# Strassen's seven block products for the second MLP product, with two attention banks and an ELU on pairs of tiles

## The chip, the cores and the metric

The kernel runs on one core of one Trainium2 chip. The metric is the device time of one execution in microseconds (us), smaller is better. The kernel before takes 628.42 us, the median of three runs (627.26 to 628.8). PE is the TensorE matmul engine, PEld its weight loads, DVE the VectorE, ACT the ScalarE, POOL the GpSimd engine.

## The reference

A gated linear attention (batch 4, 8 heads, 768 tokens, head size 48) feeds a two-layer MLP with an ELU between.

```python
f = 1.0 / (1.0 + np.exp(-f_logit))
for t in range(S):
    state = f[:, :, t, :, None] * state + np.einsum('bhd,bhe->bhde', k[:, :, t], v[:, :, t])
    y[:, :, t] = np.einsum('bhd,bhde->bhe', q[:, :, t], state)
x = y.transpose(0, 2, 1, 3).reshape(B * S, H * D)           # 3072 x 384
h = x @ w_in                                                # 384 x 2048
g = np.where(h > 0.0, h, np.exp(np.minimum(h, 0.0)) - 1.0)
out = g @ w_out                                             # 2048 x 384
```

The weights reach the core as float64 values. The kernel converts them to float32 in unit 0, with one step on ACT and three on DVE.

## The kernel before

The 3072 tokens are cut into 12 units of 256. While the MLP of unit m runs, the gates and the attention of unit m+1 are made beside it. The 2048 hidden columns are 16 tiles of 128. Unit 0 is ordered by hand. From unit 1 on a scheduler, which works with modelled durations, decides in which order the instructions stand in each engine's queue; each engine then takes its queue in order. The parts that the change and the argument touch (cuts marked):

```python
def check(n):            # 16 of them: are all weights of this piece in range?
    raw = sb.tile([128, 2 * DM], w_in.dtype, tag="raw", bufs=AHEAD, ...)      # AHEAD = 7
    nc.sync.dma_start(out=raw[:], in_=flat[n // 2])
    for i, op in enumerate((ALU.min, ALU.max)):
        nc.vector.tensor_reduce(out=spans[:, i, n : n + 1], in_=..., op=op, ...)

def decays(u, pairs, cols):                       # gates of unit u: scan, reciprocal, products
    for p in range(pairs.start, pairs.stop):
        nc.vector.tensor_tensor_scan(out=g[:, p, cols], data0=a, data1=restart[...], ...)
    nc.vector.reciprocal(p_[:, pairs, cols], g[:, pairs, cols])
    for e, x, y in ((nc.vector, t["q"], p_), (nc.gpsimd, t["k"], g)):
        e.tensor_tensor(out=x[:, pairs, cols], in0=x[:, pairs, cols], in1=y[:, pairs, cols], op=ALU.mult)

# attention in four PSUM banks: transposes and states in "t", "y"; scores and outputs in "s0", "s1"

def up(T):                                        # first product and ELU of one tile
    ph = ps.tile([128, U], FP32, tag="h", bufs=2)
    for kt in range(NKT):
        nc.tensor.matmul(ph[:], lhsT=wi[:, kt, s * 128 : (s + 1) * 128], rhs=xts[m][:, kt, :], ...)
    nc.scalar.activation(e[:], ph[:], AF.Relu, scale=-1.0)
    nc.scalar.activation(e[:], e[:], AF.Exp, scale=-1.0)
    nc.vector.scalar_tensor_tensor(out=gs[T][:], in0=e[:], scalar=-1.0, in1=ph[:], op0=ALU.add, op1=ALU.max)

def down(T):                                      # second product, in two PSUM banks
    for i in range(NW):
        nc.tensor.matmul(pms[m][i][:], lhsT=g[:, i * 128 : (i + 1) * 128], rhs=wo[:, s, :], ...)

# in the loop over the tiles s of unit m:
            up(T)
            if T >= HLAG:                         # HLAG = 2
                down(T - HLAG)
            next(steps, None)                     # one step of the gates of unit m+1
            if 4 <= m < 8 and s >= NFT - 4:
                check(4 * (m - 4) + s - NFT + 4)
```

The checks guard the conversion: if a weight is out of range, a slow general path follows. The source places them in units 4 to 7, and the scheduler pulls them forward.

## Time and profile before

| | before |
|---|---|
| median of three runs | 628.42 us |
| span of the profiled run | 626.8 us |
| PE busy | 93% of the span |
| DVE busy | 51%, but nearly full until 190 us |
| first ELU of units 0, 1, 2, 3 | 37.9, 102.5, 153.3, 201.6 us |
| steady unit | 47.0 us |

The measure is the length of a unit: the time from the first ELU of one unit to the first ELU of the next, read in DVE's timeline.

PE waits here, but only in short pieces. These are all of PE's waits between 102 and 202 us (start, length, engine, line, group, count, and in brackets the idle time before it and what ended it):

```profile
134.08 1.56 PE L749 MATMUL psH<-xt,wi 128*128 128x256 f32 x6 [1.05 <-DVE gg L757]
144.48 1.56 PE L749 MATMUL psH<-xt,wi 128*128 128x256 f32 x6 [1.15 <-DVE gg L757]
148.00 1.56 PE L749 MATMUL psH<-xt,wi 128*128 128x256 f32 x6 [0.67 <-DVE gg L757]
193.64 1.56 PE L749 MATMUL psH<-xt,wi 128*128 128x256 f32 x6 [1.00 <-DVE gg L757]
```

### The profile page before, as it was taken

The numbers are of one execution on the slowest core, as the hardware profiler recorded it, in microseconds if no ns is written. First come the engines' busy times: TensorE is split into PE (matmuls) and PEld (weight loads), VectorE is DVE, ScalarE is ACT, GpSimd is POOL, SyncE is SP. The second block draws the span as 40 slices with busy tenths as digits, with TensorE's granted clock in tenths as the row PEclk, the third lists the DMA queues.
The fourth block names the chain that finished last, engine by engine and source line by source line (L and its number), as shares of the span: only waits on it lengthen the run. The fifth ranks groups of instructions, "written<-read, shape, count | busy, mean of one in ns | idle before, by whom it ended". The sixth has DMA issues, their size and how long they took to land.

```text
span 626.8 us, 12052 instructions
## 1 busy us (share of the span) xinstructions
PE 584.9 (93%) x4922; PEld 428.7 (68%) x4922; DVE 316.6 (51%) x549; ACT 235.7 (38%) x532; POOL 55.3 (9%) x115
## 2 busy tenths in 40 slices
PE   2774989998999999999999999999999999999995
PEld 1453767766776777777777777777777777777773
DVE  6879899997796192191191192181181131131110
ACT  2252454544444424423423423423423423423332
POOL 7011012320020020020020010010000000000000
PEclk9886899999999999999999999999999999999998
DMA  8999806776772012011011011021000000000000
GB/s 185 225 258 239 203 17 144 153 250 233 268 263 57 25 53 58 26 52 33 25 52 33 25 52 32 27 52 31 27 2 7 25 2 8 27 1 8 27 0 30
DMA packets 31936, 50.71 MB, mean 81 GB/s; under 512 B 3680, under 2 KB 24704, under 8 KB 31872
## 3 DMA queue, kind: packets, MB, share of 16 engines
q1 hardware_dynamic: 31248, 49.26, 29.5%
q8 instruction: 40, 0.66, 0.5%
q10 hardware_dynamic: 624, 0.59, 0.4%
q14 instruction: 24, 0.20, 0.1%
HBM read 44.04 MB, written 4.72 MB: 78 GB/s over the span
## 4 chain that ended last, share of the span: by engine, by line
PE 77%; DVE 10%; DMA 8%; issue 2%; ACT 1%; POOL 1%; DVEq 0%; SPq 0%; POOLq 0%; ACTq 0%
PE psH L749 35%; PE psM L767 34%; DMA raw<-in_moe_w_in_dram 4%; DVE p L555 3%; DMA q<-in_q_dram 2%; DVE g L551 2%; DVE spans L524 2%; PE psS L602 2%; PE psY L639 2%; PE psT L577 2%; DMA f<-in_f_logit_dram 1%; PE psY L656 1%; DVE gg L757 1%; PE psU_t L621 1%; DVE bits L500 1%
## 5 line engine op out<-in xcount | busy, mean ns | idle before, releaser
L749 PE MATMUL psH<-xt,wi 128*128 128x256 f32 x1152 | 287.4, 386 | 11.3 <-DVE gg L757 11.2
L767 PE MATMUL psM<-wo,gg 128*128 128x384 f32 x768 | 281.7, 490 | 0.0
L749 PEld LDWEIGHTS psH<-xt,wi 128*128 128x128 f32 x1152 | 215.3, 191 | 76.7 <-DVE gg L757 19.9
L757 DVE SCALAR_TENSOR_TENSOR gg<-e,psH 128x256 f32<-128x256 f32 x192 | 79.0, 412 | 273.7 <-ACT e L755 273.6
L767 PEld LDWEIGHTS psM<-wo,gg 128*128 128x128 f32 x768 | 147.6, 192 | 62.6 <-issue 1.8
L754 ACT ACTIVATE e<-psH 128x256 f32<-128x256 f32 x192 | 73.6, 383 | 303.5 <-PE psH L749 289.7
L555 DVE RECIPROCAL p<-g 128x256 f32<-128x256 f32 x48 | 82.4, 1734 | 0.5
L755 ACT ACTIVATE e<-e 128x256 f32<-128x256 f32 x192 | 79.9, 416 | 5.9
L557 POOL TENSOR_TENSOR k<-k,g 128x256 f32<-128x256 f32 x48 | 36.3, 778 | 257.3 <-DMA k<-in_k_dram 210.7
L577 PE MATMUL psT<-ident,k 128*128 128x128 f32 x96 | 14.8, 295 | 19.6 <-POOL k L557 19.6
L551 DVE TENSOR_TENSOR_SCAN g<-f,restart 128x256 f32<-128x256 f32 x44 | 29.4, 711 | 2.7 <-POOL f L544 2.7
L524 DVE TENSOR_REDUCE spans<-again 128x1 f32<-128x768 f32 x32 | 28.8, 942 | 0.6 <-DMA again<-in_moe_w_in_dram 0.6
L577 PEld LDWEIGHTS psT<-ident,k 128*128 128x128 f32 x96 | 12.1, 152 | 24.7 <-POOL k L557 20.5
L579 ACT COPY kn<-psT 128x512 f32<-128x512 f32 x24 | 13.1, 588 | 23.0 <-PE psT L577 23.0
L557 DVE TENSOR_TENSOR q<-q,p 128x256 f32<-128x256 f32 x48 | 19.8, 432 | 0.4
L607 DVE TENSOR_TENSOR at<-psS,twice 128x512 f32<-128x512 f32 x22 | 14.1, 685 | 10.0 <-PE psS L602 10.0
L479 ACT ACTIVATE raw<-raw 128x768 int32<-128x768 uint32 x16 | 14.3, 911 | 7.7 <-DMA raw<-in_moe_w_out_dram 6.1
L540 ACT ACTIVATE f<-f 128x512 f32<-128x512 f32 x24 | 14.2, 621 | 6.3 <-DMA f<-in_f_logit_dram 5.7
L500 DVE CUSTOM_DVE_ANT_0 bits<-raw,bits 128x1536 uint16<-128x1536 uint16 x16 | 15.3, 959 | 2.4 <-ACT raw L479 1.6
L543 POOL COPY restart<-f 128x8 f32<-128x8 f32 x22 | 7.3, 332 | 101.2 <-ACT f L541 69.8
L639 PEld LDWEIGHTS psY<-at,v 64*64 64x64 f32 x704 | 11.3, 135 | 6.0 <-issue 2.7
L602 PEld LDWEIGHTS psS<-q,k 48*64 48x64 f32 x704 | 11.3, 134 | 6.0 <-issue 6.0
(65 smaller groups left out, 244.9 us busy)
## 6 DMA issues: line engine op xcount, KB each, us to landing
raw<-in_moe_w_out_dram SPq DMA_DIRECT2D x8, 768.0 KB, 11.6
again<-in_moe_w_in_dram SPq DMA_DIRECT2D x8, 768.0 KB, 6.3
again<-in_moe_w_out_dram SPq DMA_DIRECT2D x8, 768.0 KB, 7.7
v<-in_v_dram SPq DMA_DIRECT2D x12, 384.0 KB, 4.8
raw<-in_moe_w_in_dram SPq DMA_DIRECT2D x16, 288.0 KB, 9.3
out_dram<-o SPq DMA_DIRECT2D x24, 192.0 KB, 1.9
f<-in_f_logit_dram SPq DMA_DIRECT2D x23, 192.0 KB, 4.2
k<-in_k_dram SPq DMA_DIRECT2D x23, 192.0 KB, 4.3
```

What stands on the lines that cost most here:

```text
L524: nc.vector.tensor_reduce(out=spans[:, i, n : n + 1], in_=raw[:].bitcast(FP32)[:, 1::2], axis=mybir.AxisListType.X, op=op, apply_absolute_ ...
L551: nc.vector.tensor_tensor_scan(out=g[:, p, cols], data0=a, data1=restart[:, p, cols] if u else a, initial=1.0, op0=ALU.mult, op1=ALU.max,)
L555: nc.vector.reciprocal(p_[:, pairs, cols], g[:, pairs, cols])
L557: e.tensor_tensor(out=x[:, pairs, cols], in0=x[:, pairs, cols], in1=y[:, pairs, cols], op=ALU.mult)
L577: nc.tensor.transpose(pt[:, p, :], in_=qkf[u % NB]["k"][:, p, w * W : (w + 1) * W], identity=ident[:])
L602: nc.tensor.matmul(pc[r][FULL[b], w, p], lhsT=t["k"][HALF[r], p, cols], rhs=t["q"][HALF[r], p, cols], start=True, stop=True,)
L639: nc.tensor.matmul(pys[u][b][FULL[r ^ b], w, p], lhsT=vs[u % NB][FULL[b], w, h * D : h * D + 64], rhs=at[FULL[b], r, w, p], start=(w == 0 ...
L749: nc.tensor.matmul(ph[:], lhsT=wi[:, kt, s * 128 : (s + 1) * 128], rhs=xts[m][:, kt, :], start=(kt == 0), stop=(kt == NKT - 1),)
L754: nc.scalar.activation(e[:], ph[:], AF.Relu, scale=-1.0)
L755: nc.scalar.activation(e[:], e[:], AF.Exp, scale=-1.0)
L757: nc.vector.scalar_tensor_tensor(out=gs[T][:], in0=e[:], scalar=-1.0, in1=ph[:], op0=ALU.add, op1=ALU.max)
L767: nc.tensor.matmul(pms[m][i][:], lhsT=g[:, i * 128 : (i + 1) * 128], rhs=wo[:, s, :], start=(s == 0), stop=(s == NFT - 1),)
```

## The change

The second product becomes one of blocks: two tiles of the hidden layer times two halves of the 256 tokens, times two halves of the 384 output columns. Strassen's method needs seven block products instead of eight. They are summed over the whole unit in four PSUM banks, and five additions at the end of the unit assemble the output. The seven products need four sums of the activations for each pair of tiles (on DVE) and four combinations of the weights (made once, on DVE; they stand after unit 0 in the source). Units 0 and 1 keep the direct product, because the weights are still arriving. To have four banks, the attention gets two instead of four. To save DVE instructions, the ELU runs on two tiles at once. To save memory, the scan of the gates writes in place over `f`, and the range checks share three buffers of a fixed area. Two more edits come with these: all scans of a unit now stand ahead of its reciprocals, and the five attention groups stand at other tiles than the four before. The diff, cut to its core:

```diff
-    pc = [ps.tile([128, NW, HP, C], FP32, tag=f"s{r}", ...) for r in range(2)]        # scores
+    pc = [ps.tile([128, NW, HP, C], FP32, tag=f"a{r}", ...) for r in range(2)]
-    pu = [ps.tile([128, NW, HP, D], FP32, tag=n, ...) for n in ("t", "y")]            # states
+    pu = [ps.tile([128, NW, HP, D], FP32, tag=n, ...) for n in ("a0", "a1")]
...
-        raw = sb.tile([128, 2 * DM], w_in.dtype, tag="raw", bufs=AHEAD)               # a range check
+        raw = area[:, 4 + n % (AHEAD - 4)]
...
             nc.vector.tensor_tensor_scan(
-                out=g[:, p, cols], data0=a, ...
+                out=a, data0=a, ...
...
-            0: [lambda: transposed(u, 0, "t"), lambda: transposed(u, 1, "y")],
-            2: [lambda: scores(u), lambda: advance(u)],
-            4: [lambda: outputs(u)],
-            7: [lambda: carried(u)],
+            3: [lambda: transposed(u, 0, "a0"), lambda: transposed(u, 1, "a1")],
+            6: [lambda: advance(u)],
+            8: [lambda: scores(u)],
+            10: [lambda: outputs(u)],
+            12: [lambda: carried(u)],
...
+    def up(P):                                    # a pair of tiles
+        ph = ps.tile([128, 2, U], FP32, tag="h", bufs=2)
...
+        if m >= DIRECT:                           # DIRECT = 2
+            a = [[g[:, i, t * 128 : (t + 1) * 128] for i in range(2)] for t in range(2)]
+            for i, x, y, op in (
+                (0, a[1][0], a[1][1], ALU.add), (2, a[0][0], a[1][0], ALU.subtract),
+                (1, s[:, 0], a[0][0], ALU.subtract), (3, a[0][1], s[:, 1], ALU.subtract),
+            ):
+                nc.vector.tensor_tensor(out=s[:, i], in0=x, in1=y, op=op)
...
+        for bank, half, x, y in (
+            (0, 0, a[0][0], b[0][0]), (3, 0, a[0][1], b[1][0]), (2, 1, a[1][1], c[3]),
+            (1, 0, s[:, 0], c[0]), (1, 1, s[:, 2], c[2]), (0, 1, s[:, 1], c[1]), (2, 0, s[:, 3], b[1][1]),
+        ):
+            nc.tensor.matmul(pm[bank][:, half * DH : (half + 1) * DH], lhsT=x, rhs=y, ...)
...
+            add(flat[:, 0:DH], p[3][0], u2[:])    # the assembly, once a unit, five such additions
...
+            if s % 2 == 0:
+                up(P)
+            elif P:
+                down(P - 1)
...
         if m == 0:
             start.close()
+            combine()                             # the four combinations of the weights
```

## The prediction

> **What bounds the kernel now.** I read the page first: busy shares, the 40 slices, the costliest groups.
>
> ```profile
> span 626.8 us, 12052 instructions
> PE 584.9 (93%) x4922; PEld 428.7 (68%) x4922; DVE 316.6 (51%) x549; ACT 235.7 (38%) x532; POOL 55.3 (9%) x115
> ...
> PE   2774989998999999999999999999999999999995
> ...
> DVE  6879899997796192191191192181181131131110
> ```
>
> PE is full from about the fourth slice on, and DVE is full too in the first 10 to 12 slices (to some 190 us), then half idle. So there are two regimes: a start (to about 200 us) in which PE and DVE compete for the bound, and a steady stretch that is PE alone. The groups say what PE does:
>
> ```profile
> L749 PE MATMUL psH<-xt,wi 128*128 128x256 f32 x1152 | 287.4, 386 | 11.3 <-DVE gg L757 11.2
> L767 PE MATMUL psM<-wo,gg 128*128 128x384 f32 x768 | 281.7, 490 | 0.0
> ...
> L757 DVE SCALAR_TENSOR_TENSOR gg<-e,psH 128x256 f32<-128x256 f32 x192 | 79.0, 412 | 273.7 <-ACT e L755 273.6
> ...
> L555 DVE RECIPROCAL p<-g 128x256 f32<-128x256 f32 x48 | 82.4, 1734 | 0.5
> ```
>
> Each product in the program is two records (576 first-layer products, 1152 records). The mean of 490 ns is a latency; the rate is read from the timeline of PE in a steady unit:
>
> ```profile
> 382.54 1.46 PE L749 MATMUL psH<-xt,wi 128*128 128x256 f32 x6
> 383.83 1.45 PE L767 MATMUL psM<-wo,gg 128*128 128x384 f32 x4
> 385.12 1.46 PE L749 MATMUL psH<-xt,wi 128*128 128x256 f32 x6
> ```
>
> Six records start 1.29 us apart from the next group, so 215 ns for 256 columns; four take 1.29 us, so 323 ns for 384 columns. That is 0.84 ns a column plus 1 to 3 ns. A unit (256 tokens, 16 tiles of the hidden layer) is 16 x 2 x 1.294 = 41.4 us and its attention the rest of the 46.98 us period (psH at 502.84 and 549.81 in the chain of waits), so 5.6 us. No wait breaks it. The table by stage shows where that is not so:
>
> ```profile
> 140.00:190.00 50.00, 48.19 (x412) 35.16 (x411) 41.83 (x67) 23.12 (x53) 4.63 (x12) 1.00 0.71 241
> ...
> 340.00:390.00 50.00, 50.00 (x437) 37.05 (x436) 22.24 (x43) 17.68 (x43) 2.89 (x4) 1.00 0.12 35
> ```
>
> (Columns: stretch, length, PE, PEld, DVE, ACT, POOL, clock, DMA share, GB/s.) At 140 to 190 us DVE is busy 41.8 of 50 and PE already loses 2 us. The DVE timeline puts the first ELU of units 0, 1, 2 and 3 at 37.9, 102.5, 153.3 and 201.6 us: 64.6, 50.8 and 48.3 us for the first three units, against 47 us of PE work.
>
> **What the Trainium skill says.** "TensorE: Matmul & The Clock Gate", LDWEIGHTS: loading weights takes about columns/1.2 ns, 107 ns for 128 columns, and Part 2 says that the queue pulls the next load ahead of running matmuls. The trace agrees: eight 128-column transposes, each with weights of its own, take 1.04 us at 112.97, with the next group 0.87 us after their start, so 109 ns each with the load hidden. "VectorE: DVE Perf Modes", the errata section: an fp32 tensor_tensor takes (N+151)/0.96 ns. The trace: 358 ns at N=192 (formula 357), 432 at 256 (424); so I use it for sizes that are not here. "ScalarE: Activation LUTs", What ACT_TABLE_LOAD costs: with immediates, 186 + 0.833 N ns. The trace: 383 and 416 ns at 256 (399), 621 at 512 (613).
>
> **The change part by part.**
> *PE, second product.* A pair of tiles was 4 products of 384 columns, 8 records x 323 = 2.59 us. It becomes 7 products of 192 columns, 14 records of about 160 + 2.7 = 163 ns, 2.28 us. Every product now has its own weights, but a load of 107 ns fits under 163. Saved 0.31 us a pair, 2.5 us a unit, 25 us over the ten units from unit 2 on. Attention has the same products, in five groups instead of four; each switch of tile shape costs about 0.1 us. Steady unit: 16 x 1.294 + 8 x 2.28 + 5.7 = 44.6 us against 46.98; the last unit, without attention, 38.9 against 41.4.
>
> *DVE, steady.* ELU on pairs: 8 of (512+140)/0.96 = 0.68 us for 16 of 0.41, 1.2 us less. Added: 32 sums of 128 columns, 0.29 us each by the formula, 0.25 started back to back (successive DVE rows overlap by 0.07 to 0.09 us in the trace), 8.0 us; the assembly of a unit, five additions, 2.2 us. So a unit goes from about 22 to 31 us of DVE, out of 44.6. I laid the order of instructions of one steady unit against these durations: with reciprocals (1.65 us each) between, the sums of pair 3 are ready at about the time PE wants them and those of pair 4 up to 0.4 us late in some units. The assembly frees the four banks 3.2 us after the last product, and PE wants the first again after a first-layer pair and the transposes, 3.5 us. Tight, but beside PE. ACT: 16 of 0.6 us instead of 32 of 0.4, and small copies: hidden.
>
> *The first units.* Here DVE counts, so I summed DVE by unit, from the first ELU of one to the first ELU of the next, in the order that the scheduler gave, with start-to-start times of the trace (one weight conversion of three steps 2.46, scan 0.60, reciprocal 1.65, q product 0.33, state step 0.39, mask 0.6, range check 0.87, ELU 0.33, on pairs 0.60):
> - Unit 0 before: 12 conversions 29.5, 16 ELU 5.3, 8 scans 4.8, 8 reciprocals 13.2, 8 q 2.6, states and masks 4.3 = 59.7 of 64.6 us. After: two reciprocals and three q later (4.3 less), ELU 0.5 less, and 16 operations that make the four weight combinations, (384+151)/0.96 = 0.56, back to back 0.48 each = 7.6 us: 62.5. The wait of PE for the k product and the transposes (52 to 60.5 us in the trace), behind which ACT stood, goes, because both scans now come first; but DVE was busy there nearly throughout, so it gives back only a part of the 4.9 us of DVE idle. I take 65.5 us: the first ELU of unit 1, now of two tiles, at 103.5.
> - Unit 1 (still direct, PE 47): before 42.5 of DVE in 50.8. After: 10 reciprocals 16.5, 16 scans 9.6, 8 checks 7.0, 8 ELU 4.8, 11 q 3.6, rest 4.1 = 45.6. Both near PE's 47: about 51.5, so 155.
> - Unit 2 (first with seven products, PE 44.5): before 39.8 in 48.3. After: 22 checks 19.1, sums 8.0, 8 scans 4.8, ELU 4.8, reciprocals 6.6, rest 5.4 = 48.7. DVE bounds this unit: the checks of the weights' range, which filled DVE's idle time, now stand beside the sums. They also have three buffers instead of seven (landing 6 to 8 us), which can add a wait or two. About 51, so 206.
> *The end.* From there unit 3 45, 7 x 44.6, 38.9 = 396.1, so 602. The tail: the last pair cannot hide its ELU, the assembly is five dependent steps (about 2.8 us) for one copy of 0.48, and one output of 384 KB instead of two of 192 (1.9 us each); by the times of the tail before, 8.2 us after where the next ELU would be: 610.3. The runs' median is 1.6 us above the span: **612 us**. So about 9 of the 25 us saved are lost: DVE in units 1 and 2, the combinations, and the tail.
>
> **The rivals.**
> *Weights bound the seven products.* Weight loads rise from 8 to 14 a pair, and the mean LDWEIGHTS record is 192 ns, longer than 163. If that were occupancy, 14 x 192 = 2.69 us, more than before, and the kernel would end near 640. Against: the transposes' 109 ns each. Unlikely.
> *DVE stays out of the way.* Were units 1 and 2 as long as PE's work plus the earlier losses (50 and 46), the end comes near 604 to 606. For it: DVE needs no more than PE's time in unit 1. Against: unit 2's sum of 48.7 against 44.5.
> *DVE and banks stall the steady stretch.* If every unit waits 0.5 to 1 us for late sums or for the assembly's banks, 4 to 9 us: 616 to 621. For it: the slack of 0.3 us on the banks and the bunched reciprocals. Against: five of the seven products need no late sum, and the order puts the direct ones first.
> *The transfers.* The loads and the range checks moved to three buffers stand in one queue; a check that waits for its buffer holds the rows of x behind it. DMA is at 0.71 in 140 to 190. A few us in unit 2.
>
> **Range and chances.** 604 is the second rival, 621 the third. 2% faster is 615.9; my sum is 4 us below that, with an error of about 6, so faster 0.73, the same 0.25, slower 0.02 (only if the weight loads bound).
>
> **What would show it.** Right: the records of the 192-column products start 163 ns apart, the period in the steady stretch is 44.5 to 45 us with no idle time of PE; first ELU of units 1, 2, 3 near 103, 155, 206 us; DVE near full from 100 to 205 us with PE waiting for sums or ELU there; the assembly some 3 us at the end. Wrong: a period above 45.5 (late sums or banks: PE's idle time names which), a first stretch that ends before 200 or after 212, or products spaced by 190 ns.

## More of the kernel before

The page and the groups of instructions are shown in the prediction. The table by stage for units 1 and 2 adds what is needed here; its columns are the stretch in us, its length, busy time (and instructions) of PE, PEld, DVE, ACT and POOL, the granted clock of PE as a share of full speed, the DMA share, and GB/s.

```profile
102.50:153.30 50.80, 47.94 (x426) 34.66 (x425) 44.18 (x71) 26.30 (x59) 13.79 (x32) 1.00 0.72 202
153.30:201.60 48.30, 47.23 (x409) 34.60 (x408) 39.56 (x63) 22.39 (x51) 4.00 (x8) 1.00 0.61 201
```

## The result, and the profile after

| | before | after |
|---|---|---|
| median of four runs | 627.93 us | 621.72 us |
| all runs | 628.42, 628.8, 627.26, 627.44 | 622.88, 622.83, 620.6, 619.99 |
| ratio, 95% interval | | 0.9898, 0.9865 to 0.9931 |
| span of the profiled run | 626.8 us | 620.9 us |

A ratio is the mean time of one kernel's runs over the mean of the other's runs of the same rounds, so it is not quite the ratio of the medians beside it. The kernel gained 1%. All outputs are right. The measured time is 0.7 us above the top of the predicted range, and the most likely class, faster by over 2%, did not come.

The page of the kernel after, its span and its slices for DVE and for the clock of PE:

```profile
span 620.9 us, 13009 instructions
...
DVE  6879999998699976667576675483493443532432
...
PEclk9887799979999999999999999999999999999998
```

DVE is full or nearly so for longer than before: in the kernel before its slices fall to 1 or 2 between peaks, and here they stay at 5 or above until about 390 us. The clock row has low digits in the start and a 7 again in the ninth slice, at 124 to 140 us; that is in unit 1.

Of the groups, three answer to what was added: the products of a sum with a combination (three of the seven, 80 pairs, two records each, so 480), the sums (here two of the four of each pair, so 160), and the range checks, which are not new and stand in nearly the same units (before: 9 of the 32 reductions in unit 1 and 23 in unit 2; after: 8, 22, and 2 in unit 3).

```profile
L840 PE MATMUL psM<-area,sums 128*128 128x192 f32 x480 | 91.3, 326 | 0.0
...
L807 DVE TENSOR_TENSOR sums<-gg 128x128 f32<-128x128 f32 x160 | 42.5, 306 | 2.0
...
L536 DVE TENSOR_REDUCE spans<-area 128x1 f32<-128x768 f32 x32 | 29.3, 942 | 2.0 <-DMA area<-in_moe_w_out_dram 1.7
```

The steady stretch came as it was meant to. PE's timeline there:

```profile
383.34 0.81 PE L840 MATMUL psM<-wo,gg 128*128 128x192 f32 x4
383.99 0.49 PE L840 MATMUL psM<-area,gg 128*128 128x192 f32 x2
384.31 1.14 PE L840 MATMUL psM<-area,sums 128*128 128x192 f32 x6
385.29 0.49 PE L840 MATMUL psM<-wo,sums 128*128 128x192 f32 x2
385.61 2.75 PE L790 MATMUL psH<-xt,wi 128*128 128x256 f32 x12
388.20 0.81 PE L840 MATMUL psM<-wo,gg 128*128 128x192 f32 x4
```

The fourteen records of the seven products start at 383.34 and the next group at 385.61, so a pair costs 2.27 us for them, or 162 ns a record. The pair repeats after 388.20 - 383.34 = 4.86 us (4.866 on average over five periods of the last unit of no_check). The table by stage shows where the time went instead (units 1, 2 and 4):

```profile
106.20:161.10 54.90, 49.29 (x401) 35.34 (x402) 47.85 (x68) 18.90 (x36) 13.40 (x26) 0.91 0.55 151
161.10:212.50 51.40, 48.46 (x456) 42.97 (x455) 48.88 (x89) 17.71 (x33) 4.56 (x12) 0.97 0.62 194
...
259.00:303.90 44.90, 44.90 (x474) 41.20 (x474) 28.60 (x66) 15.14 (x28) 3.56 (x8) 1.00 0.17 47
```

Unit 4 is full on PE and takes 44.9 us. Unit 1 takes 54.9 us with the clock at 0.91 and DVE busy for 47.9 of them. Neither engine is full. To the first ELU of unit 3 the kernel after has lost 10.9 us (201.6 before, 212.5 after); from there to the end it gains 16.8 (626.8 - 201.6 = 425.2 against 620.9 - 212.5 = 408.4).

PE's timeline in unit 1 shows what each wait does:

```profile
122.42 1.02 PE L624 MATMUL psS<-q,k 48*64 48x64 f32 x26 [0.98 <-DVE state L608]
125.14 1.84 PE L624 MATMUL psS<-q,k 48*64 48x64 f32 x38 [1.71 <-DVE state L608]
126.92 5.43 PE L790 MATMUL psH<-xt,wi 128*128 128x256 f32 x12
...
147.74 2.75 PE L790 MATMUL psH<-xt,wi 128*128 128x256 f32 x12
152.64 4.52 PE L818 MATMUL psM<-wo,gg 128*128 128x384 f32 x8 [2.15 <-DVE gg L797]
```

The same twelve records take 2.75 us at 147.74 and 5.43 us at 126.92, right after two waits. Eight records of the direct second product take 4.52 us after a wait of 2.15; elsewhere in this unit eight take 2.74. The clock column, in small stretches around the two places, says why:

```profile
125.10:126.90 1.80, 1.76 (x38) 1.65 (x38) 1.80 (x6) 0.00 (x0) 0.39 (x1) 0.57 0.00 0
126.90:132.30 5.40, 5.40 (x15) 4.32 (x14) 5.40 (x7) 0.00 (x0) 3.06 (x4) 0.51 0.73 145
...
152.60:157.00 4.40, 4.36 (x8) 2.43 (x9) 2.40 (x3) 0.00 (x0) 0.00 (x0) 0.61 1.06 273
```

The granted clock is 0.51 and 0.61 while PE works again. The Trainium skill has this on the page "TensorE: Matmul & The Clock Gate", Part 1: after an idle window the array runs at half rate until it has been busy for a window. The trace agrees on the half rate, with the numbers above; how much idle time it takes is another matter (below). The cost of the three slow stretches, estimated, is their length times what the clock lacks: 1.8 x 0.43 + 5.4 x 0.49 + 4.4 x 0.39 = 5.1 us. PE's idle time in unit 1 is 54.90 - 49.29 = 5.6 us. So unit 1 is about 44.2 us of work at full clock (one first-layer pair of this unit ran ahead, before its first ELU), 5.6 us of waiting and 5.1 us of half speed.

The records of the clock, which the traces keep beside the instructions, show more. In all 17 traces every half-speed stretch begins on a fixed grid of 3.41 us and, but for the last one, lasts a whole number of its steps: here from 125.33 (two steps), from 152.64 (one step) and, in unit 2, from 183.36 (one step). PE was idle for 2.20 and 2.15 us of the step before the first two. So the length of a single wait does not decide, but how much of one step it fills: in spread_check (below) a wait of 2.75 us, with 2.53 of it in one step, was followed by half speed, and one of 2.88, split into 1.64 and 1.24 by a step's end, was not. This is no full rule: in the step before 183.36 PE was idle for only 0.48 us, and why the clock fell there is open.

What ACT and DVE did before the ELU that PE waited for from 150.5 us on:

```profile
145.88 0.63 ACT L796 ACTIVATE gg<-gg 128x512 f32<-128x512 f32 x1
...
148.41 1.78 DVE L536 TENSOR_REDUCE spans<-area 128x1 f32<-128x768 f32 x2
...
150.20 1.80 DVE L536 TENSOR_REDUCE spans<-area 128x1 f32<-128x768 f32 x2
151.91 1.27 DVE L797 SCALAR_TENSOR_TENSOR gg<-gg,psH 128x512 f32<-128x512 f32 x2
```

Four reductions of two range checks, 3.5 us of work that nobody needs before the last unit, stand in DVE's queue ahead of two ELUs. ACT had finished its part of the first of them at 146.51 us; DVE, which had begun another check and then ran two scans, came to it at 151.91, 5.4 us later. PE starts again 0.73 us after that. From 156.7 us on DVE itself has nothing to do for 4.36 us (until its ELU at 161.08), since PE is slow and ACT waits for PE. This is how both engines have idle time in one unit.

### The profile page after: what moved, and what is told of

Read it like the earlier page. It is cut to its first block, busy times and chain, and to the rows that moved or that the text cites. A ratio compares the mean times of both kernels' runs of the same rounds, so it can differ in the third digit from the quotient of the medians. Undisturbed runs are those within 1.5% of the kernel's fastest.

```text
span 620.9 us, 13009 instructions
## 1 busy us (share of the span) xinstructions
PE 572.7 (92%) x5402; PEld 499.3 (80%) x5402; DVE 413.4 (67%) x839; ACT 196.7 (32%) x352; POOL 59.1 (10%) x115
## 4 chain that ended last, share of the span: by engine, by line
PE 69%; DVE 14%; DMA 8%; issue 5%; POOL 1%; ACT 1%; SPq 0%; DVEq 0%; POOLq 0%
PE psH L790 33%; PE psM L840 25%; DMA area<-in_moe_w_in_dram 5%; DVE p L572 4%; PE psM L818 3%; DVE f L562 3%; DMA q<-in_q_dram 2%; PE psS L624 2%; DVE spans L536 2%; PE psU_a L643 2%; DVE gg L797 2%; PE psY L661 1%; PE psT L599 1%; PE psY L681 1%; DMA f<-in_f_logit_dram 1%
## 5 line engine op out<-in xcount | busy, mean ns | idle before, releaser
L797 DVE SCALAR_TENSOR_TENSOR gg<-gg,psH 128x512 f32<-128x512 f32 x96 | 64.8, 676 | 162.5 <-ACT gg L796 132.4
L795 ACT ACTIVATE gg<-psH 128x512 f32<-128x512 f32 x96 | 57.2, 596 | 323.6 <-PE psH L790 299.2
L840 PE MATMUL psM<-area,sums 128*128 128x192 f32 x480 | 91.3, 326 | 0.0
L572 DVE RECIPROCAL p<-f 128x256 f32<-128x256 f32 x48 | 82.5, 1734 | 0.3
L840 PEld LDWEIGHTS psM<-area,sums 128*128 128x128 f32 x480 | 80.2, 190 | 0.0
L840 PE MATMUL psM<-wo,gg 128*128 128x192 f32 x320 | 65.5, 327 | 3.5 <-DVE gg L797 3.5
L840 PEld LDWEIGHTS psM<-wo,gg 128*128 128x128 f32 x320 | 55.4, 190 | 8.3 <-DVE gg L797 4.7
L796 ACT ACTIVATE gg<-gg 128x512 f32<-128x512 f32 x96 | 60.6, 631 | 2.6
L818 PE MATMUL psM<-wo,gg 128*128 128x384 f32 x128 | 47.3, 516 | 3.3 <-DVE gg L797 3.3
L807 DVE TENSOR_TENSOR sums<-gg 128x128 f32<-128x128 f32 x160 | 42.5, 306 | 2.0
L818 PEld LDWEIGHTS psM<-wo,gg 128*128 128x128 f32 x128 | 25.3, 203 | 19.4 <-DVE gg L797 4.1
```

What stands on the lines that cost most here:

```text
L572: nc.vector.reciprocal(pts[u][:, pairs, cols], t["f"][:, pairs, cols])
L795: nc.scalar.activation(g[:], ph[:], AF.Relu, scale=-1.0)
L796: nc.scalar.activation(g[:], g[:], AF.Exp, scale=-1.0)
L797: nc.vector.scalar_tensor_tensor(out=g[:], in0=g[:], scalar=-1.0, in1=ph[:], op0=ALU.add, op1=ALU.max)
L807: nc.vector.tensor_tensor(out=s[:, i], in0=x, in1=y, op=op)
L818: nc.tensor.matmul(pm[t][:], lhsT=g[:, i, t * 128 : (t + 1) * 128], rhs=wo[:, 2 * j + i, :], start=(j == 0 and i == 0), stop=(j == NP - 1 ...
```

## The experiments

The theory was: in the first units the cost lies in **the order** in which work for later (range checks, scans, reciprocals) stands ahead of ELUs, sums and state steps in DVE's queue, not in the sum of DVE's work. The rivals were: **the sum** of DVE's work is too large there, the combinations of the weights above all; **the two attention banks** make the scores wait for the states; **the scan in place** holds the buffer of `f`; **the weight loads** bound the seven products. The last needs no experiment: the pair repeats after 4.86 us, and with loads as the bound it would have been above 5.2. Fifteen kernels ran. Unit lengths of the main ones, in us, each from the profiled run:

| unit | before | after | no_check | pin_check | pin_prepare | all_direct | late_check |
|---|---|---|---|---|---|---|---|
| 0 | 64.6 | 66.8 | 66.8 | 66.8 | 68.6 | 67.2 | 67.4 |
| 1 | 50.8 | 54.8 | 49.5 | 50.7 | 46.7 | 49.0 | 50.0 |
| 2 | 48.4 | 51.4 | 46.5 | 46.3 | 48.7 | 51.1 | 46.4 |
| 3 | 47.5 | 46.5 | 46.2 | 46.2 | 47.1 | 47.3 | 46.1 |
| 4 | 47.0 | 44.9 | 44.9 | 47.7 | 47.1 | 47.3 | 44.9 |
| 5 | 47.0 | 45.8 | 46.0 | 49.0 | 48.7 | 47.3 | 46.1 |
| 6 to 9, mean | 47.0 | 44.9 | 44.9 | 45.5 | 47.5 | 47.3 | 44.9 |
| 10 | 47.3 | 45.2 | 45.2 | 45.2 | 45.6 | 47.6 | 45.2 |

The first ELU of unit 0 lies between 37.6 and 42.0 us, and it moves from run to run without a pattern in the edits; it is left out of the comparisons.

### Without the range checks, in both kernels

```diff
     spans = cst.tile([128, 2, NFT], FP32, name="spans")
+    nc.gpsimd.memset(spans[:], 1.0)
...
-            if 4 <= m < 8 and s >= NFT - 4:
-                check(4 * (m - 4) + s - NFT + 4)
```

> The changed kernel without the range checks of the weights (32 reductions, 29 us of DVE, gone; the flag is then set from ones, the output is unchanged). Theory A, the DVE queue of units 1 and 2 is the loss: unit 2 (51.4 us in the changed kernel's trace, first ELU to first ELU) falls to 46-47, near PE's 44.9, unit 1 (54.8) to 52-53, in all 6 to 8 us less: 614-616. Theory B, the loss is in the steady stretch (banks, sums) and the throttled clock at the start: units 1 and 2 keep within 1 us, 620-621.

> The kernel before without the range checks (the control for the same edit on the changed kernel, which gave 10 us). Theory A, the checks lay in idle time of DVE before and stand in the way now: 624-626 (2 to 4 us less: units 1 to 3 from 50.8, 48.4 and 47.5 to 49, 47 and 47). If the checks cost the kernel before as much as the changed one (10 us, so 617-619), they explain nothing of the lost gain.

The kernel after without checks took 611.22 us (ratio to the kernel before of its rounds 0.9712, 0.9652 to 0.9772). The kernel before without checks took 628.32 us, beside 628.03 with them (0.9996, 0.9943 to 1.0049). So the same 32 reductions cost the kernel after 10.5 us (621.72 - 611.22, of different rounds), more than was expected, and the kernel before nothing that its runs resolve, less than was expected (in the profiled runs its units 1 and 2 together take 97.6 us without them and 99.1 with them). The table by stage of no_check for units 1 and 2:

```profile
106.20:155.70 49.50, 45.88 (x401) 33.36 (x402) 43.01 (x65) 20.75 (x39) 14.52 (x30) 0.97 0.35 74
155.70:202.10 46.40, 45.38 (x455) 40.87 (x454) 28.30 (x62) 15.88 (x29) 3.92 (x8) 1.00 0.17 46
```

The whole gain lies in these two units (5.3 and 4.9 us), and the clock is back at 0.97 and 1.00. In unit 1 DVE has only 4.8 us less to do (47.85 - 43.01), in a stretch where it was not full, and the unit is 5.3 us shorter. Not all of the 5.3 is the checks' own: PE is idle for 2.0 us less, and the clock is at half speed for one step of 3.41 us instead of three, which is worth 3.4; but one of the two steps that are gone followed a wait for state steps and not for a check. pin_check below, with no checks in unit 1 and that step still there, is 4.1 us shorter than the kernel after. This alone does not separate sum from order; the next runs go further. It is not a valid kernel, since it assumes what the checks test.

### Tied in place: the checks, the gates, both, and both in the kernel before

An instruction that copies one column of the newest ELU into the check's buffer keeps the transfer, and so the check, from being moved ahead of that ELU. The same trick through the bias of the first activation holds the gates of unit u behind the last ELU of unit u-2, that is, inside the unit where the source has them.

```diff
 # pin_check
         raw = area[:, 4 + n % (AHEAD - 4)]
+        nc.scalar.activation(raw.bitcast(FP32)[:, 0:1], gs[max(gs)][:, 0, 0:1], AF.Copy)
         nc.sync.dma_start(out=raw, in_=flat[n // 2])
 # pin_prepare
-            nc.scalar.activation(a, a, AF.Exp, scale=-1.0)
+            if u > 1 and i == 0:
+                tie = sb.tile([128, 1], FP32, tag="tie", name=f"tie{u}")
+                nc.scalar.activation(tie[:], gs[(u - 1) * NP - 1][:, 0, 0:1], AF.Copy, scale=0.0)
+                ties[u] = tie
+            if u > 1:
+                nc.scalar.activation(a, a, AF.Exp, scale=-1.0, bias=ties[u][:])
+            else:
+                nc.scalar.activation(a, a, AF.Exp, scale=-1.0)
 # pin_both: the two together; before_pinned: the same two in the kernel before
```

> The changed kernel with each range check tied to the unit in which the source puts it (units 4 to 7; its transfer first waits for a one-column copy of that unit's ELU). The same DVE work, only later. Theory A: as without checks in units 1 and 2 (6 to 8 us less), while units 4 to 8 have 38 us of DVE in 44.9 and lose at most 0.5 each: 615-618. Theory B: no gain, 621-624, as the later units get longer.

> The changed kernel with the gates of unit u+1 (and so its scans and reciprocals) tied to the end of unit u-1, so that they cannot be pulled several units ahead; the checks stay free. DVE of unit 1 falls by about 20 us of scans and reciprocals of later units. Theory A: unit 1 falls from 54.8 to 48-49 (PE 47), unit 2 stays DVE-bound by the checks at 49-51, the waits in unit 3 for the POOL (5.6 us of DVE) go: 613-616. Theory B: units 1 and 2 within 1 us of before: 620-622.

> Both ties together: the same work on every engine as the changed kernel, only in another order. Theory A: unit 1 about 47.5, unit 2 about 45.2, unit 3 about 45, units 4 to 8 about 45 to 45.5, unit 0 about 64: 604-608, so faster than both kernels. Theory B: 619-622.

> The kernel before with the same two ties (gates and range checks). If the kernel before loses in its first units to the same pulled-ahead work (units 1 to 3: 50.8, 48.3, 47.5 against 47 of PE), these become 47 each and the total 620-623. The change on top of the ties would then be worth about 16 to 18 us, not 6. If the ties do nothing for it, 627-628.

| | median us | ratio, 95% interval |
|---|---|---|
| pin_check | 624.57 | 0.9918, 0.983 to 1.0006 |
| pin_prepare | 631.01 | 1.003, 0.9971 to 1.009 |
| pin_both | 632.40 | 1.0042, 0.9962 to 1.0122 |
| before_pinned | 642.51 | 1.0214, 1.0168 to 1.0259 |

None of these is a gain (pin_both was expected at 604 to 608 us), and each says something. With the checks tied to units 4 to 7, units 1 and 2 fall to 50.7 and 46.3 us, nearly as without checks; but units 4, 5 and 7 rise from 44.9, 45.8 and 44.9 to 47.7, 49.0 and 47.1. There DVE has room by its sum: 28.6 of 44.9 us in unit 4 of the kernel after. In pin_check four checks come close together at a unit's end, beside the assembly and the first ELU: at 300.31 us DVE waits 0.74 us for a landing, reduces for 1.81, and a sum, the assembly and the ELU stand behind. So the same work costs about as much where DVE has 16 us to spare. That speaks for order and waiting, and against the sum.

With the gates tied, unit 1 falls to 46.7 us, so the scans and reciprocals of later units were a part of its loss too (the tie changes the whole order of the unit, so the part is not measured alone). But the steady units rise to 47.1 or 48.7, and pin_both, with 46.7 and 46.0 us in units 1 and 2, then has 45.3 to 50.3 in units 3 to 9. One of pin_prepare's waits in the whole run (in us: total, times, longest):

```profile
PE psM L849 <- DVE u L859: 7.5, 8, 1.0
```

L849 is the seven products and L859 the assembly: the scans now stand at the start of each unit, ahead of the assembly, and PE waits up to 1.0 us for the banks that it frees. The prediction's slack of 0.3 us on the banks was real; the scheduler's habit of running gates ahead is what kept the steady stretch free of it. The kernel before suffers likewise from ties (642.51 us): its scheduler's order was good for it.

### The arrangement without Strassen

```diff
-    DIRECT = 2
+    DIRECT = NU
...
             start.close()
-            combine()
```

> The changed kernel with the direct second product in every unit (no combinations, no sums, no assembly; all else of the change stays: pairs, two attention banks, scans in place). If PE's saving of 0.31 us a pair is real and all else costs nothing in the steady stretch, its steady period is 47.0 to 47.3 us against 44.9. Theory A (the first units' queue is the loss, combinations and sums only a part of it): units 0 to 3 lose as well by the reordering, total 630-634, 9 to 12 us over the changed kernel. If the sums and combinations alone made the loss, total 626-629.

632.25 us (1.0057, 1.0019 to 1.0094), against 629.03 for the kernel before of its rounds. The steady unit is 47.3 us, not 47.0, with PE busy throughout. So pairs, two banks and five attention groups cost 0.3 us a steady unit, and the seven products then give 47.3 - 44.9 = 2.4 us back; the predicted 8 x 0.31 is 2.5. Unit 0 is 67.2 us also without the combinations. They are thus not what made it longer than before (64.6).

This run also says something on unit 1, where it has the same direct products as the kernel after and the same eight reductions, but in another order (an ELU stands between single reductions, at 147.74 and at 149.20 us):

```profile
106.28:155.25 48.97, 45.10 (x410) 32.49 (x409) 43.03 (x61) 21.04 (x40) 12.02 (x28) 1.00 0.61 169
```

Its unit 1 takes 49.0 us instead of 54.8; the longest wait of PE is 1.29 us, and the clock stays at 1.00. DVE has 4.8 us less of other work there, so the order is not the only difference.

### The combinations on another engine

```diff
-                nc.vector.tensor_tensor(
+                nc.gpsimd.tensor_tensor(
                     out=to[:, n : n + 2], in0=x[:, n : n + 2], in1=y[:, n : n + 2], op=ALU.subtract
```

> The changed kernel with the four weight combinations made on POOL, which is idle then, instead of DVE (16 operations of 0.55 us). If DVE bounds unit 0, unit 0 (66.8 us) falls by 5 to 7 us, total 614-616. If unit 0 is bound by the arriving weights or POOL's use of SBUF slows DVE, it falls by less than 2.

627.44 us (0.9959, 0.9905 to 1.0012). Unit 0 grew to 76.1 us; units 1 and 2 were 51.2 and 49.6. One combination takes 0.99 to 1.72 us on POOL, against 0.55 on DVE, and the gates' copies for the next unit stand behind them in POOL's queue:

```profile
PE psT L599 <- POOL f L555: 7.3, 1, 7.3
```

PE's transposes waited 7.3 us once, late in unit 0, for POOL. A miss as an improvement, and the same lesson on another engine: an in-order queue delays what stands behind.

### A buffer of its own for the scan

```diff
+        gts[u] = sb.tile([128, HP, U], FP32, tag="g", name=f"g{u}")
...
-                out=a, data0=a, data1=restart[:, p, cols] if u else a,
+                out=gts[u][:, p, cols], data0=a, data1=restart[:, p, cols] if u else a,
...
-                o = sb.tile([128, 2, DM], FP32, tag="o", name=f"o{m}")
+                o = sb.tile([128, 2, DM], FP32, tag="o", name=f"o{m}", bufs=1)
```

> The changed kernel with the scan's result in a tile of its own (as in the kernel before) instead of in place over f, so that the loads of f wait no longer for the reciprocals; output tiles get one buffer in exchange. If the in-place scan matters, the 5.6 us wait of DVE for POOL in unit 3 goes and units 3 and 5 come to 45: 2 us less, 619-620. If not, 621-622.

620.75 us (0.9888, 0.984 to 0.9935), 1 us below the kernel after of other rounds. Unit 5 falls from 45.8 to 44.9 us and unit 2 from 51.4 to 49.2; unit 1 stays at 54.8 and unit 3 at 46.4. By the unit lengths the scan in place costs some 3 us, by the medians about 1, and the intervals of the two ratios overlap; so it is a small term, and its size stays uncertain.

Unit 3 therefore needs another reason, and the trace of the kernel after has it, on ACT and then PE:

```profile
244.97 1.15 ACT L551 ACTIVATE f<-f 128x512 f32<-128x512 f32 x2 [3.40 <-DMA f<-in_f_logit_dram]
...
248.88 0.58 ACT L795 ACTIVATE gg<-psH 128x512 f32<-128x512 f32 x1
...
252.56 0.92 PE L840 MATMUL psM<-wo,gg 128*128 128x192 f32 x4 [1.33 <-DVE gg L797]
```

The gates of a later unit stand in ACT's queue ahead of the ELU; they wait 3.40 us for `f` to land, the ELU's first half starts only at 248.88, and PE loses 1.33 us. In own_growth the same wait (3.07 us) is followed by 1.21 us on PE. This was read in the traces, not tested by a run.

### Free banks for the first scores

```diff
-        pc = [ps.tile([128, NW, HP, C], FP32, tag=f"a{r}", name=f"psS{u}_{r}") for r in range(2)]
+        tags = {1: ("m2", "m3"), 2: ("m0", "m1")}.get(u, ("a0", "a1"))
+        pc = [ps.tile([128, NW, HP, C], FP32, tag=tags[r], name=f"psS{u}_{r}") for r in range(2)]
```

> The changed kernel with the scores of units 1 and 2 put into the two output banks that are idle then (2 and 3 in unit 0, 0 and 1 in unit 1), so that they wait no more for the state steps that read the state update out of the two attention banks. Theory C (two attention banks: PE idle at 67-75 us and 121-127 us, each followed by half-clock matmuls, waits for state steps that stand behind reciprocals): unit 0 from 66.8 to 62-64, unit 1 from 54.8 to 50-52, total 614-617. If the units are bound by DVE's sum of work, less than 1.5 us: 620-622.

620.38 us (0.9874, 0.9824 to 0.9924). In units where two of the four banks are unused, the scores take those. Unit 1 falls to 52.4 us and unit 2 to 50.0, 3.8 us together; the first ELU of this profiled run came 2.5 us later (41.9 against 39.4), and the median is 1.3 us below that of the kernel after. The two banks are a part of the loss in unit 1: without free banks the scores wait for the state steps, which stand among reciprocals (the waits of 0.98 and 1.71 us above). They are the smaller part.

### The checks spread over eight units

```diff
+        nc.scalar.activation(raw.bitcast(FP32)[:, 0:1], gs[max(gs)][:, 0, 0:1], AF.Copy)
         nc.sync.dma_start(out=raw, in_=flat[n // 2])
...
-            if 4 <= m < 8 and s >= NFT - 4:
-                check(4 * (m - 4) + s - NFT + 4)
+            if 2 <= m < 10 and s in (8, 10):
+                check(2 * (m - 2) + (s - 8) // 2)
```

> The changed kernel with the checks tied one at a time to pairs 4 and 5 of units 2 to 9 (two checks, four reductions a unit, in the stretch in which DVE waits for the ELU's exponentials by 3 to 4 us a pair), instead of four in a row at the end of units 4 to 7. Same DVE work. Theory A (it is the place in DVE's queue, not the sum): units 1 and 2 as without checks (49.5, 46.5), steady units 45.0-45.4, total 611-614. Rival (DVE cannot take the checks beside the sums wherever they stand, as the run with tied checks seems to say): each unit 1 to 1.5 us longer, 619-622.

> Three edits together: checks spread, scores in free banks, the scan's result in its own tile. If they are independent, spread_check's gain plus scores_free's plus about 1: 605-610. If the bank edit does nothing, 610-613.

spread_check took 625.65 us (0.998, 0.9898 to 1.0062); spread_free_own, which adds the free banks and the scan's own buffer, 630.78 (1.0045, 0.9995 to 1.0094). This was the plainest miss: two checks a unit, well apart, should have been hidden. DVE's waits between 204 and 520 us in spread_check show why not:

```profile
DVE spans L537 <- DMA area<-in_moe_w_out_dram: 20.4, 5, 4.8
DVE spans L537 <- DMA area<-in_moe_w_in_dram: 15.0, 7, 4.4
```

The tie lets the transfer start only just ahead of its reduction. The reduction then waits up to 4.8 us for the landing, 35.4 us in all, with ELUs and sums behind it; PE waited 2.75 and 2.88 us for an ELU at 246.29 and 296.20. The cost of these checks was the wait, not the 0.94 us of a reduction.

### The checks placed late, with their transfers early

```diff
+            if 2 <= m < 10 and s == 0:
+                for n in range(2):
+                    fetch_check(2 * (m - 2) + n)      # tied to the newest ELU, then the transfer
+            if 2 <= m < 10 and s in (11, 13):
+                check(2 * (m - 2) + (s - 11) // 2)    # tied to the last sum of the newest pair
...
         for i, op in enumerate((ALU.min, ALU.max)):
+            nc.scalar.activation(spans[:, i, n : n + 1], ss[max(ss)][:, 3, 0:1], AF.Copy)
             nc.vector.tensor_reduce(
```

late_check_own adds the scan's own buffer, and late_own_free the free banks as well.

> The changed kernel with the two halves of a range check tied apart: two transfers at the start of each of the units 2 to 9, and the reductions only after the last sum of pairs 5 and 6 of the same unit, some 25 us later, so that DVE should not wait for a landing. Same DVE work. Theory A in its last form (checks cost where they stand ahead of an ELU or wait for a landing, not by their sum): units 1 and 2 as without checks (49 to 50 and 46.5), steady units 44.9 to 45.3, no wait of DVE for a transfer, total 611-614. Rival (any reduction beside sums and reciprocals costs PE about its own length, 1.8 us a check): units 46 to 47, total 618-624.

> late_check with the scan's result in its own tile. If that takes away the waits of DVE for POOL in units 3 and 5 as in the run of that edit alone: 1 us under late_check, 610-613.

> late_check_own with the scores of units 1 and 2 in idle banks. By the run of the bank edit alone (unit 1 2.4 us shorter, unit 0 none): 608-612; if there it only moved checks about, as late_check_own.

| | median us | ratio, 95% interval |
|---|---|---|
| late_check | 615.60 (6 runs) | 0.9773, 0.9732 to 0.9814 |
| late_check_own | 614.29 (6 runs) | 0.9761, 0.9724 to 0.9798 |
| late_own_free | 615.39 (4 runs) | 0.9806, 0.9758 to 0.9854 |

Now all 16 checks are done, on the same engine, and by the unit lengths they hardly cost anything: units 1 to 10 take 458.2 us together, 457.8 in no_check and 468.2 in the kernel after. The median is still 4.4 us above that of no_check, of other rounds; in the profiled runs 3.8 of 4.2 us lie in the start, unit 0 and the tail, and why is not explained. The table by stage of late_check, units 1, 2 and 4:

```profile
108.40:158.30 49.90, 45.79 (x401) 33.35 (x402) 43.45 (x64) 20.74 (x39) 14.44 (x30) 0.97 0.35 74
158.30:204.70 46.40, 45.46 (x456) 40.88 (x455) 31.81 (x66) 16.48 (x36) 3.94 (x8) 1.00 0.27 80
...
250.80:295.70 44.90, 44.90 (x475) 41.20 (x474) 32.28 (x70) 15.81 (x34) 3.57 (x8) 1.00 0.28 83
```

Unit 4 carries two checks, DVE is busy 32.3 us in it instead of 28.6, and it still takes 44.9 us with PE full. Units 1 and 2, now with no check and with two, are nearly as short as without any (50.0 and 46.4 against 49.5 and 46.5). Against the kernel after, the work of the whole run is the same and the place is not, so the total of DVE's work was not the limit. The sum within one unit is not excluded by this: unit 2 had 22 of the 32 reductions, and DVE was busy for 48.9 of its 51.4 us. What separates the sum within a unit from order and waiting is late_check beside spread_check, whose unit 4 is this:

```profile
254.40:302.70 48.30, 45.42 (x475) 41.14 (x474) 32.09 (x71) 15.31 (x30) 3.69 (x8) 1.00 0.25 77
```

Both have two checks in each of the units 2 to 9. DVE is busy 32.1 us there and 32.3 in late_check, and the unit takes 48.3 us and 44.9. late_check_own is the fastest valid kernel, 2.4% below the kernel before (its interval lies wholly under 0.98) and about 7 us below the kernel after. The free banks give nothing more once the checks are out of the way (unit 1 is 51.7 us in late_own_free, 50.0 in late_check_own).

## Why the prediction was right or wrong

The prediction was wrong in size: 612.0 against 621.72 us, with the class "faster" at 0.73 and the class "same" observed. Term by term, in the profiled span (610.3 predicted, 620.9 measured, 10.6 us apart):

| term | predicted | measured | miss |
|---|---|---|---|
| start, first ELU of unit 0 | 37.9 | 39.4 | +1.5 |
| unit 0 | 65.5 | 66.8 | +1.3 |
| unit 1 | 51.5 | 54.8 | +3.3 |
| unit 2 | 51 | 51.4 | +0.4 |
| unit 3 | 45 | 46.5 | +1.5 |
| units 4 to 10 | 7 x 44.6 | 315.4 | +3.2 |
| last unit and tail | 47.1 | 46.5 | -0.6 |

**The saving on PE was right.** "Saved 0.31 us a pair" is what the pair's period shows (4.86 us) and what all_direct confirms (2.4 us a unit). The rival of the weight loads fell, as its chance said. The signs of being right came for the steady stretch (162 ns a product record, a period of 44.9 us). For the start its own sign of being wrong came: the first ELU of unit 3 stood at 212.5 us, after 212. Three slips in the working change nothing: 0.84 ns a column is already the whole of the 215 and 323 ns, with nothing to add; 16 x 0.48 is 7.7 us, not 7.6; and the rival of the weight loads comes to 645 us by its own figures, not 640.

**The largest failed step is unit 1**: "Both near PE's 47: about 51.5". It added up DVE's work, found 45.6, and allowed 4.5 us over PE's time. DVE's sum was right in kind (47.9 us measured) and it did fit; the step that failed is that two engines that both fit would then overlap. What was missing is a term for the order in the queue and one for the clock. PE waited 5.6 us for ELUs and state steps that stood behind checks and reciprocals, and the half speed after those waits cost another 5.1. In units 1 and 2 the kernel before has waits of the same kind, but none above 1.15 us, at a clock of 1.00. Its start does show the second cost: after the wait of 5.30 us that ends at 60.52, six first-layer records at 61.64 take 2.77 us instead of 1.46, and the clock is at 0.50 from 61.85 to 64.40. The prediction saw that wait and did not carry this cost over.

**Unit 2 came out right (51.4 against 51), in part by luck.** "DVE bounds this unit" is what its busy time says (48.88 of 51.4), and without the checks it falls to 46.5. But 2.9 us of it are PE's waits and 1.7 the half-speed step at 183.36, which the sum did not have. And the work that filled it need not have stood there: late_check carries all checks and has 46.4.

**The range checks were mis-sized.** The prediction named them, counted 8 reductions in unit 1 and 22 in unit 2, as the trace has them, and put them into the DVE sums. Beside its second rival (50 and 46 us) it gives units 1 and 2 together 6.5 us for this; without the checks they are 10.2 us shorter. The second rival ("DVE stays out of the way", 604 to 606) takes their hiding for a matter of DVE's sums, though it is a matter of where they are placed. Even without them the time is 611.2 us, so that rival was out of reach by this cause alone.

**The other terms.** Units 4 to 10 miss as much together as unit 1 alone (3.2 us). The steady units were 0.3 us longer than 44.6: eight pairs are 8 x 4.866 = 38.9, so the attention takes 6.0 us and not 5.7. all_direct, with the same five attention groups, shows the same: 47.3 less the 41.4 us of its products is 5.9. Unit 5 (45.8) is the scan in place, removed in own_growth. Unit 3 is the gates on ACT waiting for their load. In the rival "DVE and banks stall the steady stretch" 616 to 621 us was the right time for the wrong place; the steady stretch did not stall, except when pin_prepare made it.

**Open.** What bounds unit 0 at about 67 us is not settled: DVE is busy 64.4 of 66.8 us, but all_direct, with 61.5 us of DVE work there, takes 67.2. The spread of the start (37.6 to 42.0 us) is not explained. Why the kernel before loses little or nothing by its checks, which stand in the same units, is argued and not tested: its DVE has 39.6 us of work in the 48.3 us of unit 2, and its waits come singly, for one tile. That the place of the checks costs the time in unit 1 is read in the trace and borne out by all_direct; no run changes their order within unit 1 and nothing else. In unit 2 the sum within the unit remains a rival.

## What to carry to other kernels

When a change fills an engine that had room, ask not only whether its work still fits by the sum, but what stands ahead of the instructions that the bound engine waits for: an engine's queue is in order (in pin_check a sum whose input was ready at 299.3 us ran at 302.04, behind a check that waited for its landing), and work that is needed only at the end does harm where it stands at the front. Tie such work to a place with room, and start its transfer well before that place. And look whether a wait of PE is followed by a low clock: here one of 2.15 us cost another 1.8. Whether it is depends on where in the 3.41 us grid the wait falls, so the same wait can be dear in one run and cheap in another.

## What the Trainium skill lacked or had wrong

- "TensorE: Matmul & The Clock Gate", Part 1, gives an idle window of about 3.4 us before the clock falls. Here a window need not be idle throughout: one with 2.15 us of idle time was enough, the next 3.41 us ran at half clock, and eight records took 4.52 us instead of 2.74. Waits of 1.0 to 1.15 us in units 1 and 2 of the kernel before left the clock at 1.00.
- The same page, Part 1, gives columns / 2.4 ns plus about 2.5 ns from one matmul to the next at full clock, which is 109 ns for 256 columns; its runs are in bf16, and the figure does not carry over to fp32. Here each fp32 product is two records, and each record takes 0.84 ns a column: 215 ns for 256 columns, 323 for 384, 162 for 192.
- No page gives the time of a reciprocal on DVE. From start to start one took 1.65 us for 128x256 fp32 elements.
